# The output projection of a memory-augmented attention by column tile: 128 outputs per tile over all heads, with a block transpose into the next segment

## The chip, the cores and the metric

The kernel runs on one core of a Trainium2 chip. The metric is the device time of one execution in microseconds, lower is better. Engines are named TensorE (PE; its weight loads PEld), VectorE (DVE), ScalarE (ACT), GpSimd (POOL) and SyncE (SP, which here only issues DMAs).

## The reference, cut to what matters

Two attention branches on the same x (2048 tokens, 512 features, bf16) are mixed by a gate per token. Branch A goes through 64 segments of 32 tokens one after the other and hands 8 memory rows on:

```python
mem = mem0                                        # 8 rows
for s in range(64):
    h = concat([mem, x[32*s : 32*(s+1)]])         # 40 tokens
    q, k, v = h @ Wq, h @ Wk, h @ Wv              # 32 heads of 128
    p = softmax(where(mask, q @ k.T * scale, -1e9))
    o = einsum('hqe,hed->qd', p @ v, Wo)          # 40 rows of 512
    mem, out[s] = o[:8], o[8:]
```

Branch B is a 32-head attention of head size 16 in four blocks of 512 tokens, with a running compressive memory; it has no serial chain through A. The result is `g * A + (1 - g) * B`, with `g = sigmoid(x . gate_w)`.

So a segment of A can't begin before the first 8 output rows of the segment before are known.

## The kernel before, in words

**Phases.** The first 61 us load the inputs, transpose x into `xT` and make B's projections. After that branch A runs in 16 groups of four segments; B's attention steps, the left-over rows and the output of earlier groups are put between A's steps. Everything is unrolled.

**The order.** A segment's work is cut into units, and three written lists (`A_FIRST` for groups 0 to 2, `A_GROUP`, `A_LAST`) give the order in which units are issued; a unit that has nothing to do is skipped. Each engine works its own instructions in that order, and semaphores carry the dependencies. Names in the lists: `0.K0x` is segment 0's K projection, half b=0 of the heads, first half of the contraction; `k0` its eviction, `TK0` its transpose; `S` scores, `X` exponentials, `M` sums, `L` reciprocals, `N` and `n` norms (`n` on GpSimd), `PV`/`PL` values, `E` evictions into `OT_sb`, `W` the output projection, `H` its eviction, `F` the fold, `hm` the memory rows into the next segment's `hT`, `ax` the output rows, `xc` the copy of x into `hT`, `oL` and `qt` copies of left-over rows. `bS`, `bE`, `bP`, `bT` are B's scores, exponentials, values and late steps, `tb` and `tf` the output of an older group, `tl` its loads.

**Left-over rows.** A segment has 40 rows, of which the 32 column tiles' rows hold the 8 memory rows and the first 24 tokens. The last 8 tokens of four segments are treated together as one further tile of 32 rows: `left_units(g)` makes their K, Q and V (`KL0` ... `VL1`) for the next group while a group runs, `ol0`/`ol1` their output projection.

**Column tiles.** TensorE is used as four column tiles of 32: a stationary operand of 128 x 32 makes 32 output partitions, and four matmuls with neighbouring tiles run side by side. In `out_part` (line 1087) tile j takes head 4k+j with all 512 outputs:

```python
for k in ks:
    for j in range(4):
        matmul(pb[bk][32*j : 32*(j+1), :], lhs(4*k + j), Wo_sb[:, 4*k + j, :], ...)
```

So each tile holds a part sum over 8 of the 32 heads. `part_out` evicts the bank in two halves to f32 (`WF`, or `LN_sb` for the left-over rows), and `fold` (line 1105) adds the four parts and turns the rows into columns with small f32 matmuls against a 0/1 matrix; `w_mem` and `w_rows` evict what is needed into `hT` and `aT_st`.

**Left values.** The left-over V is evicted to `LN_sb`, block-transposed into `VTL`, turned by 16 matmuls against the identity (`vt0`, `vt1`, line 1066) and evicted into `VL`. Before group 0 all eight left units run one after the other.

Of the kernel before, what the change touches and what calls it, by code (L numbers as in the profile page):

```python
# [233 lines left out]
def build(nc, es, A_x, A_mem0, A_Wq, A_Wk, A_Wv, A_Wo, B_wq, B_wk, B_wv, B_wo, B_beta, gate_w, out, dbg=None):  # L234
# [31 lines left out]
    def alloc(stack, *specs):  # L266
        at, spans = 0, {}
        for name, shape, dt, n in specs:
# [10 lines left out]
    alloc(es, ("ident", [128, 128], BF16, 0), ("xT", [128, C, S], BF16, 0), ("hT", [128, C, SEG], BF16, 2),  # L279
# [9 lines left out]
          ("aTg", [128, C, 128], BF16, 0), ("fold", [128, SEG], F32, 0), ("VTL", [128, 4, H // 2, 8, 2], BF16, 0),  # L289
          ("WF", [128, DM], F32, 0))  # L290
    esP = ExitStack()
    in_p = alloc(esP, ("wkB", [128, C, DM], BF16, 0), ("wqB", [128, C, DM], BF16, 0), ("phK", [128, 4, DM], BF16, 0), ("etmp", [128, 512], BF16, 5),
          ("bmask", [128, 136], BF16, 0), ("mskT", [128, 2, 2, 8, 2], BF16, 0), ("mem0_sb", [128, DM], BF16, 0), ("gwr_sb", [128, 128], BF16, 0), ("beta_sb", [128, HB], BF16, 0),
# [6 lines left out]
    RT = [128, 4, H // 2, 8, 2]  # L300
    in_a = alloc(esA, ("xL", [128, C, SEG], BF16, 0), ("LN_sb", [128, 2, 512], BF16, 0), ("KTL0", RT, BF16, 0), ("QTL0", LT, BF16, 0), ("VL0", [128, 2, 512], BF16, 0),
          ("KN_sb", [128, 2, 512], BF16, 0), ("QN_sb", [128, 2, 512], BF16, 0), ("KT_sb", LT, BF16, 0), ("QT_sb", [128, H // 2, L, 2], BF16, 0),
          ("V_sb", [128, 2, 512], BF16, 0), ("P_sb", [128, 2, 224], BF16, 0), ("R_sb", [128, 2, 160], F32, 0),
          ("OT_sb", [128, H, L], BF16, 0), ("OTL", [128, H, SEG], BF16, 2), ("KTL1", RT, BF16, 0), ("QTL1", LT, BF16, 0), ("VL1", [128, 2, 512], BF16, 0),
          ("oTt", [128, 16, 32], F32, 0), ("t1_sb", [128, DM], F32, 0), ("aT_st", [128, C, 128], BF16, 2))
# [12 lines left out]
    dram("aTd", [NG, 128, C, 128])  # L318
# [97 lines left out]
def plan_const(v):  # L416
# [29 lines left out]
    def late():  # L446
# [5 lines left out]
        for n in range(2):  # L452
            gp(lambda g, n=n: g.memset(v.mskT[:, n, n, :, :], 0.0), rmt, "mskT0")
        rf = Rs("fold")
        gp(lambda g: g.memset(v.fold[:], 0.0), rf, "fold0", True)
        for j in range(4):
            sel(v.fold[:], [[-1, SEG]], ALU.not_equal, 1.0, -SEG * j, 1, rf, "fold1_%d" % j)
        for j in range(4):
            q = slice(32 * j, 32 * j + 32)
            gp(lambda g, q=q: g.memset(onesb[q, q], 1.0), rob, "onesb1_%d" % j)  # L460
            for i in range(4):
                o = (L + 16) * i
                sel(mneg[q, o + M:o + L], [[1, 32]], ALU.is_ge, NEG, M, -1, rmk, "mneg1_%d" % j)
            for n in range(2):
                row = v.mskT[q, n, n, :, :]
                for u in range(2):
                    sel(row[:, :, u], [[-1, 8]], ALU.is_ge, NEG, -16 * u - 8, 1, rmt, "mskT1_%d" % j)
                    sel(row[:, :, u], [[0, 8]], ALU.is_ge, 0.0, -16 * u - 8, 1, rmt, "mskT2_%d" % j)
                    sel(row[:, :, u], [[0, 8]], ALU.is_ge, NEG, -16 if u else 15, 1 if u else -1, rmt, "mskT3_%d" % j)
        v.late_mask = lambda: P.op("dve", lambda d: d.transpose(mneg[:, :].rearrange("p (i w) -> p i w", w=L + 16)[:, :, L:L + 16], v.mskT[:, :, :, :, :].rearrange("p n m k u -> p (n m) (k u)")),  # L470
# [4 lines left out]
def plan_warm(v):  # L475
    P, Rs, BK = v.P, v.Rs, v.BK
    v.warm = v.WF[:, :].bitcast(BF16)[:, 0:512]
# [94 lines left out]
def gate_parts(v):  # L572

    P, Rs, BK, C, NTT = v.P, v.Rs, v.BK, v.C, v.NTT
    st = {}
# [25 lines left out]
    def memory():  # L601
# [8 lines left out]
        v.evac("dve", v.hT[0][:, :, 0:v.M], v.pb16[bk][:, 0:C * v.M].rearrange("p (c t) -> p c t", t=v.M), [bk], [Rs("hTm0_0"), Rs("hTm0_1")], "memT0")  # L610
# [136 lines left out]
class BAttn:  # L747
# [178 lines left out]
A_FIRST = """  # L926
    bP bP bT bS 0.Q0x tl bE tl bE 0.Q0y 0.K0x 0.K0y 0.Q1x tb tf 0.q0 bE bT 0.qt 0.Q1y 0.K1x 0.k0 0.K1y 0.TK0 0.q1 bP 0.TQ0 bP 0.TQ1 0.k1 bS 0.V0x 0.S0
    bP bP 0.TK1 0.V0y 0.S1 0.V1x 0.X0 0.V1y 0.M0 QL1 0.X1 0.M1 bE bT 0.v1 0.L0 tbe 0.n0 0.v0 0.N0 tbe VL0 0.xc tf 0.L1 0.PV0 bT tfe 0.PL0 0.n1 KL1 bP
    0.N1 0.E0b 0.E0a 0.PV1 0.PL1 0.W0b 0.E1a 0.E1b 0.W0a 0.W1a tf 0.W1b bP VL1 bT 0.H0 0.F0 tf 0.H1 0.F1 bT tfe 0.hm0 0.hm1 QL0 tl 0.ax0 0.ax1 tf bS
    1.Q0x 1.Q0y 1.K0x 1.Q1x 1.q0 1.K0y bE 1.K1x bE 1.K1y 1.Q1y 1.qt bP 1.k0 1.TQ0 tf 0.oL 1.k1 bE bP 1.TK0 bS tl 1.TK1 bP 1.S0 1.q1 tf 1.V0x 1.TQ1 bS  # L930
    1.V1x 1.S1 bP 1.X0 tb 1.M0 bE 1.V0y 1.X1 tfe 1.M1 bT tb tb 1.L0 tfe bE 1.v0 1.V1y tf 1.N0 1.L1 bP tbe bE 1.n0 1.PV0 1.xc bE 1.n1 1.PL0 QL1e 1.E0b
    1.N1 KL0 1.v1 1.E0a 1.PV1 1.PL1 1.W0b 1.E1a 1.E1b 1.W0a bT 1.W1a tbe 1.W1b 1.H0 bS tb bT tfe 1.F0 1.H1 tl 1.oL tl 1.hm0 1.F1 1.hm1 bP 2.qt 2.Q0x
    1.ax0 2.K0x 2.Q0y tbe bT bE bT bS 1.ax1 bE 2.K0y 2.k0 2.Q1x VL1e tfe 2.Q1y bT 2.K1x 2.K1y 2.q0 2.q1 2.TQ0 2.TK0 2.S0 VL0e 2.k1 tl bP tb bP tfe
    2.TQ1 KL1e bS 2.TK1 2.V0x tb 2.X0 bS tl KL0e 2.M0 2.S1 2.V0y 2.V1x ol0 2.L0 2.X1 bP 2.M1 tbe tf 2.n0 2.V1y 2.v0 2.N0 bE 2.PV0 2.PL0 tl 2.L1 2.E0a
    2.v1 2.E0b ol1 bP 2.n1 tb 2.N1 tb 2.PV1 tfe 2.PL1 ol1e 2.W0a 2.E1a 2.E1b 2.W0b 2.W1a 2.W1b vt0 2.H0 bE bS tb tb bT tbe 2.F0 2.H1 2.hm0 2.F1 3.qt
    2.hm1 bP 2.xc 3.K0x vt0e 2.ax0 3.Q0x bP tf bP 3.K0y 3.Q0y bP tfe 3.Q1x 3.K1x 3.Q1y 2.ax1 3.q0 bS 3.k0 bP 3.K1y 3.V0x 3.q1 tl 2.oL 3.TQ0 3.TK0 3.k1
    tf 3.S0 3.X0 3.TQ1 3.TK1 bE 3.V0y 3.V1x 3.S1 3.M0 3.X1 3.V1y 3.L0 3.v0 tfe of bE 3.M1 3.v1 3.L1 3.n0 3.N0 3.PV0 3.N1 3.n1 3.PL0 3.E0a bE 3.xc bE
    3.PV1 3.PL1 3.W0a 3.E1b QL0e 3.E0b 3.E1a 3.W0b 3.W1b 3.W1a vt1 bS bE bE 3.H0 3.F0 3.H1 tl 3.F1 vt1e bP tbe 3.hm0 3.ax0 3.hm1 bS bT 3.oL tf tf ofe
    3.ax1
    """.split()  # L940
A_GROUP = """
    bE tl bE bP 0.K0x 0.Q0x 0.K0y 0.Q1x 0.Q0y 0.K1x bT 0.qt 0.K1y 0.k0 0.TK0 0.q0 0.TQ0 0.Q1y 0.V0x 0.V1x 0.S0 bE 0.k1 tb 0.q1 0.TK1 0.V0y 0.TQ1 0.X0
    0.S1 tf 0.v0 0.X1 0.M0 0.V1y 0.M1 tb 0.L0 0.L1 tbe tfe KL0 0.N0 bT 0.n0 0.v1 bT 0.PV0 bE 0.N1 0.PL0 KL1 0.xc 0.E0b 0.E0a bP 0.PV1 0.n1 0.PL1 tbe
    0.W0b 0.W0a tfe 0.E1a 0.E1b 0.W1b 0.W1a 0.H0 bE QL1 0.F0 bS bP bT 0.H1 0.F1 0.hm0 0.ax0 1.qt 0.hm1 1.K0x 1.Q0x 1.Q0y 1.K0y 1.K1x 0.ax1 1.Q1x 1.K1y
    bE 1.q0 1.Q1y 1.TQ0 1.k0 1.TK0 1.k1 1.S0 VL0 1.q1 1.TK1 bE 1.V0x 1.TQ1 0.oL 1.X0 1.S1 tfe bE 1.M0 tb tbe VL0e 1.X1 1.V0y 1.M1 1.L0 1.n0 1.V1x 1.v0
    1.N0 1.V1y 1.L1 tbe 1.PV0 1.N1 KL0e 1.PL0 tf tf 1.E0a bP bE vt0 tb tbe 1.E0b 1.v1 tf 1.n1 1.PV1 1.PL1 1.W0a 1.E1a vt0e 1.E1b 1.W0b bT 1.xc 1.W1b
    1.W1a QL1e bE bT bP 1.H0 1.H1 1.F0 tfe bS tb 1.hm0 1.F1 1.ax0 1.hm1 2.Q0x 2.Q1x 1.ax1 bE bT 2.K0x 2.Q0y bP 2.K0y 2.K1x bT 2.K1y bE tb 2.q0 2.Q1y
    bE 2.qt 2.k0 1.oL bP bP 2.TQ0 2.TK0 tb 2.S0 2.k1 2.TK1 2.q1 bS 2.TQ1 VL1 2.X0 2.M0 2.S1 bE tb 2.L0 VL1e 2.V0x 2.X1 tfe 2.V0y 2.V1x 2.n0 bE 2.M1
    2.V1y 2.N0 2.v0 bT 2.PV0 2.v1 2.L1 tbe 2.N1 2.PL0 QL0 2.E0a 2.E0b 2.n1 KL1e bP 2.PV1 2.PL1 tfe 2.W0b 2.E1b 2.W0a 2.E1a 2.W1b 2.W1a bP QL0e 2.H0
    2.H1 ol0 bE 2.F0 3.qt 2.F1 2.xc bT 2.hm0 bS 2.hm1 3.Q1x bS 2.ax1 3.Q1y 2.oL 3.K1x 3.K0x 3.q1 3.K1y 3.k1 3.Q0x 3.K0y 3.TQ1 3.TK1 3.Q0y 3.V1x bE tb  # L950
    3.S1 3.k0 3.V1y 3.q0 3.X1 3.TQ0 3.V0x 3.M1 3.L1 3.V0y 2.ax0 3.TK0 3.v1 3.N1 3.S0 3.n1 ol1 3.v0 3.X0 3.M0 3.PV1 tb 3.xc 3.PL1 tb 3.E1b 3.L0 tl vt1
    3.E1a tb 3.N0 3.n0 3.PV0 vt1e 3.PL0 ol1e 3.W1b 3.E0a tfe bT bE 3.E0b 3.W1a 3.W0b 3.W0a 3.oL of bS tfe tbe 3.H0 3.F0 3.H1 tl ofe tfe 3.F1 3.hm0 bP
    bT 3.hm1 3.ax0 3.ax1 bS
    """.split()
A_LAST = """
    bP tl bE bS bE 0.Q1x 0.K1x 0.K1y bP tb 0.Q1y bP bE 0.K0x 0.qt bP 0.K0y 0.k1 bS 0.TK1 0.Q0x 0.q1 bE 0.TQ1 bE 0.Q0y 0.S1 bS tl 0.k0 0.V1x tl 0.V0x
    0.X1 0.TK0 bE 0.M1 bE tbe 0.q0 tb tbe bS 0.TQ0 0.V1y bE bP 0.v1 0.L1 0.S0 0.V0y bE 0.n1 tf bP 0.N1 bE tf 0.X0 bE 0.M0 tl tb 0.PV1 tbe bT tf 0.PL1
    tb tbe 0.v0 tb bS tf ol0 0.L0 tl 0.E1a 0.E1b 0.xc tl tbe bT 0.n0 0.N0 0.PV0 bP 0.PL0 0.W1a bS 0.W1b tf bE tb 0.E0a 0.W0a 0.E0b 0.W0b tbe ol1 0.H0
    bT bE bP 0.F0 tbe 0.H1 0.hm0 0.F1 0.hm1 1.Q0x tf 1.Q0y bP 0.ax0 1.qt 1.K0x 1.K0y 1.K1x tb bE 1.Q1x tl 1.K1y bP bE bP bP bP bE 1.q0 tb 1.k0 1.Q1y
    tfe 1.TQ0 tb 1.TK0 tfe ol1e 1.V1x tf tf tf 1.k1 1.q1 1.V0x 1.S0 1.xc bP tfe bP bP 1.TK1 tb bT tbe bT 1.V1y 1.TQ1 bP tf 1.X0 bS bE 1.S1 1.X1 tf  # L960
    1.M0 bT 1.V0y tl bP 1.v1 0.ax1 1.v0 1.L0 2.qt 0.oL bE 1.M1 tfe 1.L1 1.N0 tb 1.N1 1.n0 1.PV0 tb tfe 1.PL0 bP 1.n1 bT 1.PV1 1.E0a 1.PL1 tfe 1.E1b bP
    bP bT 1.W0a bT bE tbe 1.E0b bE tb 1.W0b bT bP tb tb bE bE 1.E1a 1.W1b tfe tbe 1.W1a bP of bS 1.H0 bE ofe 1.F0 bT 1.H1 tb 1.F1 1.oL bS 1.hm0 bS
# [572 lines left out]
```

## Time and profile before

| | us |
|---|---|
| three runs, median | 860.64 |
| lowest and highest | 859.37 and 860.79 |
| the profiled execution | 859.77 |
| its span, first to last instruction | 858.0 |
| TensorE busy (matmuls) | 825.7 |
| ScalarE busy | 579.4 |
| VectorE busy | 572.7 |
| GpSimd busy | 254.4 |

How to read it: busy time is the union of an engine's instructions. Matmuls are pipelined and their ends are modelled, so the busy time of TensorE says that it had something to do, and not that it ran at its peak. In group lines, "xN | busy, mean of one in ns | idle before, and what ended it" stand in this order. In window lines each engine has busy time and, in brackets, the number of its instructions that lie in the window; waits for a semaphore are not in that number.

### The profile page before, as it was taken

To read this page: it belongs to the slowest core of one execution; us is meant where nothing else is said; L and a number is where in the kernel's file an instruction comes from. 1 tells how busy PE (TensorE), PEld (TensorE's weight loads), DVE (VectorE), ACT (ScalarE), POOL (GpSimd) and SP (SyncE) were. 2 spreads that over 40 slices of the span, in tenths; PEclk is the share of its full clock that TensorE was granted. 3 is DMA by queue.
4 is the path that set the end of the run, shared out by engine and by line. 5 is a ranking of instruction groups with operands and counts; after the bars stand their busy time and mean duration, and the time that the engine had idled before them with its cause. 6 is when DMAs were issued, how large, how long until landed. Compare 5 with 4: busy or idle time off the path is not lost.

```text
span 858.0 us, 51309 instructions
## 1 busy us (share of the span) xinstructions
PE 825.7 (96%) x23047; PEld 451.5 (53%) x23054; DVE 572.7 (67%) x1219; ACT 579.4 (68%) x1412; POOL 254.4 (30%) x619
## 2 busy tenths in 40 slices
PE   8998999999999999999999999999999999999997
PEld 4644454555555555555655555555555555565554
DVE  3856566565676767676776767677676767677654
ACT  5764876776677676767676676767677676767554
POOL 3611332323242232323232323233233223223210
PEclk9999999999999999999999999999999999999999
DMA  9997110000011010111111010111101011110011
GB/s 325 390 391 267 23 41 22 17 25 21 24 35 30 16 44 13 32 32 33 30 31 28 21 31 26 33 33 32 29 22 38 20 27 32 32 43 4 16 47 40
DMA packets 63587, 51.34 MB, mean 60 GB/s; under 512 B 33920, under 2 KB 59784, under 8 KB 61832
## 3 DMA queue, kind: packets, MB, share of 16 engines
q1 hardware_dynamic: 61640, 35.48, 14.4%
q10 hardware_dynamic: 1728, 12.58, 3.7%
q8 instruction: 181, 2.97, 1.4%
q14 instruction: 38, 0.31, 0.1%
HBM read 33.47 MB, written 14.57 MB: 56 GB/s over the span
## 4 chain that ended last, share of the span: by engine, by line
PE 88%; ACT 5%; DMA 3%; DVE 2%; issue 1%; POOL 0%; SPq 0%; DVEq 0%; ACTq 0%; POOLq 0%
PE ps L1007 46%; PE ps L1087 17%; PE ps L1105 4%; PE ps L1319 3%; PE ps L652 2%; PE ps L811 2%; PE ps L863 2%; PE ps L1175 2%; PE ps L1289 2%; PE ps L1258 1%; PE ps L1255 1%; DMA scr_kqd<-stgk 1%; PE ps L676 1%; DVE V_sb L365 1%; ACT R_sb L1299 1%
## 5 line engine op out<-in xcount | busy, mean ns | idle before, releaser
L837 POOL TENSOR_SCALAR_AFFINE_SELECT PT<-PT 128x256 bf16<-128x256 bf16 (+2 forms) x160 | 88.6, 554 | 271.0 <-ACT PT L830 265.9
L830 ACT ACTIVATE PT<-ps 128x1024 bf16<-128x1024 f32 x160 | 161.6, 1026 | 6.7 <-PE ps L811 5.9
L1007 PE MATMUL ps<-Wq_sb,hT 128*32 128x512 bf16 x2048 | 145.2, 380 | 0.4 <-ACT hT L363 0.3
L1007 PE MATMUL ps<-Wv_sb,hT 128*32 128x512 bf16 x2048 | 141.8, 379 | 0.8 <-issue 0.5
L1007 PE MATMUL ps<-Wk_sb,hT 128*32 128x512 bf16 x2048 | 140.6, 379 | 0.0
L1087 PE MATMUL ps<-Wo_sb,OT_sb 128*32 128x512 bf16 x2048 | 124.5, 380 | 0.3 <-issue 0.2
L363 ACT ACTIVATE OT_sb<-ps 128x320 bf16<-128x320 f32 x192 | 76.7, 434 | 50.5 <-PE ps L1331 48.0
L365 DVE CAST V_sb<-ps 128x512 bf16<-128x512 f32 x128 | 87.1, 683 | 23.4 <-PE ps L1007 22.9
L363 ACT ACTIVATE KN_sb<-ps 128x512 bf16<-128x512 f32 x128 | 77.0, 601 | 33.7 <-PE ps L1007 31.3
L1309 POOL TENSOR_TENSOR P_sb<-P_sb,R_sb 128x64 bf16<-128x64 bf16 x128 | 50.4, 394 | 143.8 <-ACT R_sb L1299 131.9
L1019 DVE STREAM_TRANSPOSE KT_sb<-KN_sb 128x256 f32<-128x256 f32 x128 | 56.3, 440 | 54.8 <-ACT KN_sb L363 54.3
L363 ACT ACTIVATE WF<-ps 128x256 f32<-128x256 f32 x128 | 42.2, 381 | 72.3 <-PE ps L1087 72.3
L1007 PEld LDWEIGHTS ps<-Wk_sb,hT 128*32 128x32 bf16 x2048 | 55.2, 97 | 49.8 <-ACT PT L830 3.0
L1007 PEld LDWEIGHTS ps<-Wq_sb,hT 128*32 128x32 bf16 x2048 | 54.1, 96 | 49.8 <-ACT hT L363 2.6
L365 DVE CAST QN_sb<-ps 128x512 bf16<-128x512 f32 x64 | 43.7, 684 | 52.7 <-PE ps L1007 52.7
L1019 DVE STREAM_TRANSPOSE QT_sb<-QN_sb 128x256 f32<-128x256 f32 x128 | 56.8, 444 | 26.3 <-ACT QN_sb L363 22.3
L1087 PEld LDWEIGHTS ps<-Wo_sb,OT_sb 128*32 128x32 bf16 x2048 | 48.5, 96 | 45.9 <-DVE OT_sb L365 8.7
L1272 ACT ACTIVATE P_sb<-ps 128x224 bf16<-128x224 f32 x128 | 45.6, 356 | 26.5 <-PE ps L1289 12.6
L365 DVE CAST LN_sb<-ps 128x512 bf16<-128x512 f32 x80 | 54.3, 678 | 9.7 <-PE ps L1007 8.7
L1007 PEld LDWEIGHTS ps<-Wv_sb,hT 128*32 128x32 bf16 x2048 | 46.4, 96 | 27.0 <-ACT KN_sb L363 2.2
L365 DVE CAST OT_sb<-ps 128x320 bf16<-128x320 f32 x64 | 31.4, 491 | 37.3 <-PE ps L1331 36.1
L1319 PEld LDWEIGHTS ps<-P_sb,V_sb 32*128 32x128 bf16 x2048 | 23.4, 91 | 51.9 <-ACT OT_sb L363 24.4
(132 smaller groups left out, 1450.8 us busy)
## 6 DMA issues: line engine op xcount, KB each, us to landing
Wk_sb<-in_A_Wk_dram ACTq DMA_DIRECT2D x4, 1024.0 KB, 7.5
scr_kqd<-stgk SPq DMA_DIRECT2D x16, 256.0 KB, 7.5
Wq_sb<-in_A_Wq_dram ACTq DMA_DIRECT2D x4, 1024.0 KB, 7.9
Wv_sb<-in_A_Wv_dram ACTq DMA_DIRECT2D x4, 1024.0 KB, 7.8
Wo_sb<-in_A_Wo_dram SPq DMA_DIRECT2D x8, 512.0 KB, 6.9
scr_vd<-V SPq DMA_DIRECT2D x16, 136.0 KB, 6.7
Vj<-scr_vd SPq DMA_DIRECT2D x32, 68.0 KB, 2.4
Wo_sb<-in_A_x_dram SPq DMA_DIRECT2D x8, 256.0 KB, 6.5
```

The costliest lines, as they stand in the source:

```text
L363: P.op("act", lambda a: a.activation(dst, src, ACT.Copy), reads=[v.rbank[k] for k in bks], writes=dres, name=name)
L365: P.op("dve", lambda d: d.tensor_copy(dst, src), reads=[v.rbank[k] for k in bks], writes=dres, name=name)
L652: ins = pe.matmul(v.pb[bk], w[:, c, f * 128:(f + 1) * 128], v.xT[:, c, 512 * sb:512 * (sb + 1)], start=(c == 0), stop=(c == C - 1))
L830: P.op("act", lambda a: a.activation(pt[:, :, :], v.ps[:, bks[0]:bks[1] + 1, :], ACT.Exp, scale=v.SCALE_B), reads=[v.rbank[b] for b in bks ...
L837: P.op("gp", lambda g: g.affine_select(mv, mv, [[0, 2], [0, len(cut)], [1, 128]], ALU.is_ge, 0.0, base=0, channel_multiplier=-1), reads=[r ...
L1007: ins = pe.matmul(pb[bk][SEG * j:SEG * (j + 1), :], lhs(c), cols(w, j) if split else w[:, 512 * j:512 * (j + 1)], start=(c == 0), stop=(c ...
L1019: P.op("dve", lambda d: d.transpose(to, src), reads=reads, writes=writes, name=name)
L1087: ins = pe.matmul(pb[bk][SEG * j:SEG * (j + 1), :], lhs(4 * k + j), Wo_sb[:, 4 * k + j, :], start=(first and k == ks[0]), stop=False, skip ...
L1105: ins = pe.matmul(pb[bk][SEG * j:SEG * (j + 1), SEG * n:SEG * (n + 1)], part[:, o:o + SEG], v.fold[:, :], start=True, stop=True, skip_grou ...
L1272: P.op("act", lambda a: a.activation(P_sb[:, b, :], pb[bk][:, 0:224], ACT.Exp, scale=SCALE), reads=[rbank[bk]], writes=[Rs("P%d" % b), Rs( ...
L1309: P.op(ENG["n"], lambda d: d.tensor_tensor(left(P_sb), left(P_sb), grp04(R_sb[:, b, :]), ALU.mult), reads=[Rs("R%d" % b)], writes=[Rs("P%d ...
L1319: ins = pe.matmul(pb[bks[j]][:, L * i:L * (i + 1)], V_sb[SEG * j:SEG * (j + 1), b, i * E:(i + 1) * E], P_sb[SEG * j:SEG * (j + 1), b, LW * ...
```

## The change

**Output projection.** Each head now goes to all four column tiles: tile j takes 128 of the 512 outputs, so that the bank holds finished sums over all heads, 32 rows of tokens by 128 outputs in each tile. A segment has 128 matmuls with 128 columns where it had 32 with 512.

```diff
             for k in ks:
-                for j in range(4):
-                    ins = pe.matmul(pb[bk][SEG * j:SEG * (j + 1), :], lhs(4 * k + j), Wo_sb[:, 4 * k + j, :],
-                                    start=(first and k == ks[0]), stop=False, skip_group_check=True)
+                for i in range(4):
+                    h = 4 * k + i
+                    for j in range(4):
+                        ins = pe.matmul(pb[bk][SEG * j:SEG * (j + 1), 0:128], lhs(h), cols(Wo_sb[:, h, :], j),
+                                        start=(first and k == ks[0] and i == 0), stop=False, skip_group_check=True)
```

**No folds.** `part_out`, `fold`, `folded` and the constant `fold` go. One eviction (ScalarE for segments, VectorE for left-over rows) writes pairs of bf16 into `WN`, and one VectorE block transpose of 32-bit elements writes them into the next segment's `hT`, which has a new layout with pairs of contraction rows next to each other:

```diff
+    def row_ev(bk, name, eng):
+        evac(eng, v.WN[:, :, :, :].rearrange("p k e u -> p k u e"), pb[bk][:, 0:128].rearrange("p (k u e) -> p k u e", u=2, e=SEG),
+             [bk], [Rs("WN")], name)
+        B.give(bk)
+
+    def out_turn(dst, writes, name):
+        src = v.WN[:, :, :, :].rearrange("p k e u -> p k (e u)").bitcast(F32)
+        P.op("dve", lambda d: d.transpose(dst, src), reads=[Rs("WN")], writes=writes, name=name)
...
-        lhs = lambda c: hT[s % 2][:, c, 0:SEG]
+        lhs = lambda c: hT[s % 2][:, c // 2, 0:4, :, c % 2].rearrange("p a q -> p (a q)")
...
+            out_turn(hT[nxt][:, :, 0::4, :, :].bitcast(F32)[:, :, :, :, 0], [Rs("hTm%d" % nxt), Rs("hTa%d" % nxt)], "hm%d" % s)
...
+            P.op("gp", lambda gq: gq.tensor_copy(dst, src), reads=[Rs("hTa%d" % nxt)], writes=[Rs("aTx%d_%d" % (par, r))], name="atx%d" % s)
```

The output rows now go from `hT` to `aT_st` by a GpSimd copy (`ax`), and `x_copy` is two GpSimd copies, one for each parity.

**Left values.** V's left-over rows are evicted without a transpose into `VNL`, stored to DRAM by one DMA and read back, turned, by four; `vt0` and `vt1` go. The rows of a left-over tile are ordered by token and then segment, so `flip_rows` for K has two half-sized transposes.

```diff
+        def turn_values():
+            P.dma(P.group("vs%d" % g, "vs"), lambda s: s.dma_start(v.vld[g].rearrange("p b a e -> p b (a e)"), v.VNL[:, :, :]),
+                  reads=[Rs("VNL0"), Rs("VNL1")], writes=[Rs("vld%d" % g)], name="stl%d" % g)
+            grp = P.group("vl%d" % g, "vl")
+            rows = v.vld[g].rearrange("(q r) b a e -> a q (r b) e", r=4)
+            for a in range(4):
+                P.dma(grp, lambda s, a=a: s.dma_start(VL[par][a:128:4, :, :], rows[a]),
+                      reads=[Rs("vld%d" % g)], writes=[Rs("VL%d_%d" % (par, b)) for b in range(2)], name="ldl%d_%d" % (g, a), scratch=True)
```

**Lists.** Sixteen lists, one a group, take the place of three; the first also holds the left units of group 0 (`iKL0` ... `iVL1e`), which ran ahead of it. The turns of group 9, as the lists have them (`...` for other units):

```diff
+    ... 0.W1a 0.E1b 0.W1b 0.H 0.hm bS ol1e bP bP 0.oL bE 1.qt bT bE 1.Q0x 1.Q0y 1.q0 ...
+    ... 1.W1a 1.W1b 1.H KL1 bS 1.hm 1.ax 2.K0x 2.Q0x ...
+    ... 2.W1a 2.W1b 2.H 2.hm 2.ax bT bS 3.xc 3.Q0x 3.Q0y bE ...
+    ... 3.W0a 3.W0b 3.W1a 3.W1b 3.H 3.hm 3.ax
```

Masks, `KTL`, `QTL` and `aT_st` change their layout to match.

## The prediction

> **What bounds the kernel now.** I read the page first, for shares and the instruction queue.
>
> ```profile
> PE 825.7 (96%) x23047; PEld 451.5 (53%) x23054; DVE 572.7 (67%) x1219; ACT 579.4 (68%) x1412; POOL 254.4 (30%) x619
> ...
> q8 instruction: 181, 2.97, 1.4%
> ```
>
> TensorE is busy 96%, no other engine over 68%. Each matmul has a weight load of its own, so TensorE runs 46,101 instructions; queue 8 brings them: 2.97 MB in 181 packets are 16 KB each, that is 256 instructions of 64 bytes.
>
> Next the groups by form on TensorE, for what the change touches.
>
> ```profile
> L1087 PE MATMUL ps<-Wo_sb,OT_sb 128*32 128x512 bf16 x2048 | 124.5, 380 | 0.3 <-issue 0.2
> L1105 PE MATMUL ps<-fold,WF 128*32 128x32 f32 x2048 | 37.1, 199 | 4.6 <-ACT WF L363 2.8 <-issue 0.9 <-DVE aT_st L365 0.3
> L1066 PE MATMUL ps<-ident,VTL 128*32 128x128 bf16 x512 | 12.9, 220 | 1.1 <-DVE VTL L1024 1.1
> ```
>
> Four column tiles run side by side, so the mean of one says little; what a run costs is the step from its first row to the next run's in the timeline of TensorE.
>
> ```profile
> 410.49 1.03 PE L1087 MATMUL ps<-Wo_sb,OTL 128*32 128x512 bf16 x16
> 411.35 0.27 PE L1289 MATMUL ps<-P_sb,onesb 128*32 128x160 bf16 x8
> ...
> 411.80 0.41 PE L1066 MATMUL ps<-ident,VTL 128*32 128x128 bf16 x16
> 412.03 1.04 PE L1175 MATMUL ps<-woB_sb,oTg 128*32 128x512 bf16 x16
> ...
> 415.19 0.45 PE L1105 MATMUL ps<-fold,LN_sb 128*32 128x32 f32 x32
> 415.57 0.40 PE L811 MATMUL ps<-QTj,KTj 32*128 32x256 bf16 x8
> ```
>
> Sixteen 512-wide matmuls take 0.86 us (a round of four 0.216), sixteen 128-wide ones 0.23 (a round 0.056 between starts), a fold of 32 takes 0.38. TensorE streams at full rate; the granted clock is 1.00.
>
> The timeline also has short waits in TensorE for which nothing visible is due ("issue"), in mid-run. Windows from 0 to two of them count instructions:
>
> ```profile
> 0.00:416.70 416.70, 398.11 (x10372) 213.66 (x10379) 273.52 (x579) 285.68 (x666) 129.67 (x338) 1.00 0.28 92
> 0.00:465.46 465.46, 445.92 (x11769) 240.93 (x11777) 307.72 (x652) 319.12 (x749) 144.35 (x371) 1.00 0.26 85
> ```
>
> Matmuls and loads between them: 2795, and 21 waits of TensorE's own (line 212): 2816, exactly 11 x 256. The waits at 77.7, 376.7, 509.8, 514.4, 709.1 and 757.5 us also lie whole multiples of 256 from these. So TensorE stands at the seam of two 16 KB blocks until the next block is there. At such a wait the packet for the block after starts 1.1 to 2.2 us later, takes 1.04 us, and the seam behind it opens at the earliest 1.2 us after it has landed. Blocks that ended in such a wait took 3.7 to 4.6 us; the quickest that did not, 2.9 (I take it that TensorE was then still working off a queue of older instructions). Cut into blocks at every alignment, the trace's steps lack 3.0 us in all to a least block time of 3.4 us, 4.5 us to 3.5; the loads' waits at seams sum to about 4. I take 3.4 us as the least time of a block of 256, bounds 3.0 and 3.7. Before, a block takes 4.6 on average and hardly meets it.
>
> **Part by part**, against the profiled execution's 859.8 us (span 858.0 and 1.8 around it; 0.9 under the median).
>
> *Folds and value turns leave TensorE.* Folds: 64 x 0.385 + 16 x 0.385 = 30.8 us; value turns 32 x 0.234 = 7.5. All of it stands in TensorE's stream: -38.3.
>
> *Wo.* Before, a segment has 32 matmuls in 8 rounds: 1.74 us. After, each head goes to all four column tiles with 128 outputs: 128 matmuls in 32 rounds, at the value turn's 0.056 1.79 us. The strided 128 columns cost nothing: Wk's and Wq's matmuls read so, and take 380 ns against Wv's 379. 64 segments and 16 left-over products, each again 128 for 32: 80 x 0.055 = +4.4.
>
> *The turn to the next segment.* Before: last Wo matmul, two evictions, folds, evictions into hT, projection.
>
> ```profile
> 550.44 0.66 ACT L363 ACTIVATE WF<-ps 128x256 f32<-128x256 f32 x2 [0.87 <-PE ps L1087]
> ...
> 551.58 0.34 ACT L363 ACTIVATE hT<-ps 128x16 bf16<-128x16 f32 x2 [0.47 <-PE ps L1105]
> ```
>
> In the shortest turns the chain takes 1.5 us from the last Wo matmul's start, and what TensorE does in it leaves some 0.7 us of waiting a group, 11 in all. After: 0.22 (drain of a 128-wide matmul) + 0.05 hop + one ScalarE eviction of 128 columns (0.275, between the rows of 64 at 0.224 and 160 at 0.300) + hop + one VectorE block transpose of 64 f32 columns (0.245: 256 take 0.444, 64 bf16 take 0.239) + hop = 0.89 us. The new lists put under it bS and two bP at the first turn of a group (0.6 us), at the others mostly one bS (0.22 to 0.32): 0.2 + 0.6 + 0.6 + 0.5 = 1.9 us less an odd left projection, 20 in all: +9.
>
> *Instruction blocks.* Added: 96 matmuls a segment and 96 a group, each with its load: 15,360 instructions; gone: 2560 folds and 512 value turns with loads, 6144. 55,300 remain, about 217 blocks. What counts is density: Wo's 256 instructions are exactly one block's worth and would run in 1.79 us. A segment has about 840: projections 192 in 5.2 us, scores 112 in 0.5, sums 32 in 0.24, values 80 in 0.47, left projections 48 in 1.3, left Wo 64 in 0.45, the other branch's rest. With these and 0.37 us of softmax waits a segment (before: 24 us) laid in the written order of groups 5 to 13, a block that starts with Wo's first instruction takes 1.9 us and lacks 1.46 to 3.4. One that starts 128 earlier has the values (80 instructions, 0.47, with 0.37 of waits), some 48 others mostly of projections (1.2) and half of Wo (0.9): 2.96, and lacks 0.45 on the mean. In the same way 64 earlier lacks 0.89, 64 later 0.68, 128 later 0.27 (behind Wo the thin projections begin: 32 instructions in 0.86 us); the eight other positions of a segment 0.67 together. Each position, 64 apart, has a weight of a quarter of a segment: 4.42 / 4 = 1.1 us a segment, 64 times = 70 us; the 4 of before are in its span already: +66. Ends: at 3.0 us some 40, at 3.7 some 105. I stay at 3.4, which the trace of before reproduces. [...]
>
> *Left values through DRAM.* Two VectorE evictions (684 ns) and two transposes a group go from VectorE. SyncE gains one store and four loads, each holding the queue 0.3 to 0.6 us; the loads wait for the store to land, and behind them stand the other branch's K and Q loads, needed only a step later. Store 1.8 + load 2.5 to landing and five issues: some 6 to 8 us, against about 10 us of list between VL1e and the next group's PL0: 0, at most 1 us a group (16).
>
> *GpSimd* gains a second copy for xT (0.25 us) and the row copies: 254 becomes some 290 us. Cover: it sits idle 132 us for the softmax reciprocals alone; if that is gone, norm_left comes 0.25 us late, up to 16 us. *VectorE and ScalarE* lose 25 and 73 us net, off the path: 0. Layouts of masks, KTL and QTL: 0.
>
> *Start and end.* From the first left projection (61.1 us) to the first segment's (70.9), 4.1 us are waits. After, Wv's landing (66.9) still gates, and the first values' DRAM round trip falls into full DMA queues (6.7 us to land): 3.4 us of waits, bounds 0 and 8: -0.7. End: one fold chain less: -1.
>
> Sum: 859.8 - 38.3 + 4.4 + 9 + 66 - 0.7 - 1 = 899.2, say **900 us**.
>
> **Rivals.** (A) *The blocks arrive in time.* Then the sum is 833 us, 3% faster. For it: the stream of TensorE does shrink by 34 us, and 2.9 us blocks passed without a wait. Against: every long "issue" wait lies on the 256 grid. It decides by the least block time: below about 2.8 us the change gains, above it the waits eat the gain. Chance 0.20.
> (B) *Part:* sequencer running ahead hides about half: 845 to 869. Chance 0.10.
> (C) *Values late too:* blocks as forecast, PL0 waits 1 us a group and GpSimd delays the norms: 900 + 32 = 932. For it: five DMAs in a row on one queue. Against: some 10 us of lead. Chance 0.05.
> (D) The change does what it says; a merged weight load for the four tiles, which would halve the added instructions, is excluded by the projections: there four neighbours share one stationary operand, and 2048 matmuls have 2048 loads. No chance given.
>
> **Numbers.** Forecast 0.65 with its own range 870 to 930 (block time 3.0 to 3.6, start and turn terms). Leaving out most of A and C, the range is 848 to 930. A difference of 0.2% is about what a measurement of this kernel can tell: faster A and a little of B, 0.22; same 0.02; slower 0.76.
>
> **What would show it.** Right: queue 8 with about 217 packets; "issue" waits before Wo's or the next rows, on the 256 grid, 60 to 80 us in all; Wo runs of 128 broken in the middle; the fold rows gone; unbroken Wo runs of 1.8 us. Turn waits on hT's transpose of some 0.5 us. Wrong: whole Wo runs back to back with blocks under 2.8 us apart, or a main wait on VL's loads, or rounds of Wo slower than 0.056.

## The result: 955 us for 861, and the profile after

The changed kernel takes 954.98 us (four runs, 951.39 to 958.17), the kernel before beside it 860.71. The ratio is 1.108, 95% interval 1.101 to 1.115. The forecast was 900 us, with a range up to 930: the direction was right, the size was not.

The page of the profile after, engines and instruction queue:

```profile
span 956.3 us, 60594 instructions
PE 833.8 (87%) x27655; PEld 504.2 (53%) x27662; DVE 561.0 (59%) x1218; ACT 533.7 (56%) x1095; POOL 284.7 (30%) x742
q8 instruction: 217, 3.56, 1.5%
```

Queue 8 brings the 217 blocks that were forecast. TensorE is now busy 87% and no other engine more than 59%: it waits, and not for them. What it waits for is in the waits after, matmuls first, then weight loads (us in total, times, longest):

```profile
PE ps L1214 <- issue: 50.7, 46, 2.0
PE ps L1138 <- DVE hT L1226: 9.7, 25, 0.7
PE ps L808 <- issue: 8.1, 6, 1.9
PE ps L1433 <- DMA VL<-scr_vld: 7.5, 1, 7.5
PE ps L1138 <- issue: 6.3, 11, 1.3
```

```profile
PEld ps L1214 <- issue: 61.6, 61, 2.2
...
PEld ps L1138 <- issue: 18.3, 39, 1.8
```

L1214 is Wo. Its "issue" waits stand in the middle of a run, as the timeline after shows:

```profile
406.28 1.97 PE L1214 MATMUL ps<-Wo_sb,OT_sb 128*32 128x128 bf16 x128
...
419.65 0.46 PE L1214 MATMUL ps<-Wo_sb,OT_sb 128*32 128x128 bf16 x20
421.51 1.24 PE L1214 MATMUL ps<-Wo_sb,OT_sb 128*32 128x128 bf16 x76 [1.40 <-issue]
...
442.49 0.22 PE L1365 MATMUL ps<-QT_sb,KTL 128*32 128x32 bf16 x7 [0.82 <-issue]
...
469.00 0.57 PE L1214 MATMUL ps<-Wo_sb,OTL 128*32 128x128 bf16 x26 [1.22 <-issue]
```

An unbroken run of 128 lasts 1.97 us with the last matmul's own 0.2, so a round is 0.056 us, as costed. The runs at 419.65 and 469.00 are cut. Windows from one cut to the next count the instructions between:

```profile
421.40:442.40 21.00, 19.31 (x637) 11.94 (x637) 13.65 (x32) 12.41 (x25) 7.98 (x19) 1.00 0.11 27
442.40:468.90 26.50, 24.38 (x893) 15.08 (x892) 16.43 (x35) 14.78 (x33) 8.32 (x21) 1.00 0.12 32
```

With TensorE's own 6 and 7 semaphore waits these are 1280 and 1792 instructions, 5 and 7 blocks of 256. Over the whole trace the weight loads' waits on this grid are 95.6 us in 96 places (before: 4.9 in 14). The new steps of the turn cost what was put down for them, 0.316 (0.275) and 0.245 us (0.245):

```profile
L364 ACT ACTIVATE WN<-ps 128x128 bf16<-128x128 f32 x64 | 20.2, 316 | 125.6 <-PE ps L1214 115.5
L1226 DVE STREAM_TRANSPOSE hT<-WN 128x64 f32<-128x64 f32 x63 | 15.5, 245 | 115.7 <-ACT WN L364 115.7
```

The second surprise is at the start: the first Wo run ends at 98.4 us, before at 83.2 (an end is here the start of the run's last matmul). SyncE's timeline after:

```profile
80.45 1.62 SPq L521 DMA_DIRECT2D Wo_sb<-in_A_Wo_dram  x2
82.11 1.26 SPq L1170 DMA_DIRECT2D scr_vld<-VNL  x1
89.37 2.50 SPq L1175 DMA_DIRECT2D VL<-scr_vld  x4
```

The store of the first left values stands behind Wo's eight loads of 0.5 MB; it is issued at 82.11, has landed at 89.3, and the loads land at 93.6.

But 8.1 of these 15.2 us are lost before there is a left value to store. The left V projection, which makes the values, starts at 74.94 us, before at 66.87:

```profile
37.32 0.69 DVE L638 SCALAR_TENSOR_TENSOR stgp<-stgk,etmp 128x512 bf16<-128x512 bf16 x1 [5.45 <-DMA scr_pQd<-stgp]
74.94 1.91 PE L1138 MATMUL ps<-Wv_sb,xL 128*32 128x512 bf16 x32 [0.43 <-DMA Wv_sb<-in_A_Wv_dram]
```

In wideplus (below), whose code up to there is that of after, the same projection starts as early as before:

```profile
66.23 1.91 PE L1138 MATMUL ps<-Wv_sb,xL 128*32 128x512 bf16 x32
```

In this execution of after, VectorE waits 5.45 us, until 37.3, for a store of branch B to land; wideplus has no such wait there. So the 8 us are a difference between executions, and not shown to come from the change. It goes both ways: narrow, which starts with the code of before, begins its left V projection at 72.6 us.

### The profile page after: what moved, and what is told of

Read it like the earlier page. It is cut to its first block, busy times and chain, and to the rows that moved or that the text cites. A ratio compares the mean times of both kernels' runs of the same rounds, so it can differ in the third digit from the quotient of the medians.

```text
span 956.3 us, 60594 instructions
## 1 busy us (share of the span) xinstructions
PE 833.8 (87%) x27655; PEld 504.2 (53%) x27662; DVE 561.0 (59%) x1218; ACT 533.7 (56%) x1095; POOL 284.7 (30%) x742
## 4 chain that ended last, share of the span: by engine, by line
PE 61%; issue 8%; ACT 3%; DVE 2%; POOL 0%; ACTq 0%; DVEq 0%
PE ps L1138 35%; PE ps L1214 14%; PE ps L1421 2%; PE ps L1276 2%; PE ps L1391 1%; PE ps L860 1%; PE ps L808 1%; PE ps L1357 1%; PE ps L1360 1%; ACT WN L364 1%; DVE hT L1226 1%; PE ps L1365 1%; PE ps L1433 1%; ACT OT_sb L364 0%; PE ps L1296 0%
## 5 line engine op out<-in xcount | busy, mean ns | idle before, releaser
L1214 PE MATMUL ps<-Wo_sb,OT_sb 128*32 128x128 bf16 x8192 | 144.6, 221 | 42.8 <-issue 41.7
L827 ACT ACTIVATE PT<-ps 128x1024 bf16<-128x1024 f32 x160 | 156.7, 1021 | 35.5 <-PE ps L808 21.5
L1214 PEld LDWEIGHTS ps<-Wo_sb,OT_sb 128*32 128x32 bf16 x8192 | 121.7, 97 | 61.6 <-issue 50.5
L1138 PE MATMUL ps<-Wq_sb,hT 128*32 128x512 bf16 x2048 | 137.7, 382 | 9.8 <-DVE hT L1226 7.0
L1138 PE MATMUL ps<-Wk_sb,hT 128*32 128x512 bf16 x2048 | 131.4, 380 | 4.3 <-DVE hT L1226 2.7
L364 ACT ACTIVATE OT_sb<-ps 128x320 bf16<-128x320 f32 x192 | 77.3, 433 | 78.4 <-PE ps L1433 70.0
L364 ACT ACTIVATE WN<-ps 128x128 bf16<-128x128 f32 x64 | 20.2, 316 | 125.6 <-PE ps L1214 115.5
L1226 DVE STREAM_TRANSPOSE hT<-WN 128x64 f32<-128x64 f32 x63 | 15.5, 245 | 115.7 <-ACT WN L364 115.7
L1138 PEld LDWEIGHTS ps<-Wv_sb,hT 128*32 128x32 bf16 x2048 | 49.6, 95 | 26.3 <-issue 4.5
L1405 DVE TENSOR_TENSOR P_sb<-P_sb,R_sb 128x160 bf16<-128x160 bf16 x128 | 43.6, 341 | 31.0 <-ACT R_sb L1401 24.6
L1398 ACT ACTIVATE R_sb<-ps 128x160 f32<-128x160 f32 x128 | 38.7, 302 | 40.8 <-PE ps L1391 40.6
```

The source lines that it names most:

```text
L364: P.op("act", lambda a: a.activation(dst, src, ACT.Copy), reads=[v.rbank[k] for k in bks], writes=dres, name=name)
L827: P.op("act", lambda a: a.activation(pt[:, :, :], v.ps[:, bks[0]:bks[1] + 1, :], ACT.Exp, scale=v.SCALE_B), reads=[v.rbank[b] for b in bks ...
L1138: ins = pe.matmul(pb[bk][SEG * j:SEG * (j + 1), :], lhs(c), cols(w, j) if split else w[:, 512 * j:512 * (j + 1)], start=(c == 0), stop=(c ...
L1214: ins = pe.matmul(pb[bk][SEG * j:SEG * (j + 1), 0:128], lhs(h), cols(Wo_sb[:, h, :], j), start=(first and k == ks[0] and i == 0), stop=Fal ...
L1226: P.op("dve", lambda d: d.transpose(dst, src), reads=[Rs("WN")], writes=writes, name=name)
L1398: P.op("act", lambda a: a.activation(R_sb[:, b, :], pb[bk][:, 224:384], ACT.Ln), reads=[rbank[bk]], writes=[Rs("R%d" % b)], name="ln%d_%d" ...
```

## The experiments

### Wo in wide matmuls again, in the kernel after (wide)

```diff
-                for i in range(4):
-                    h = 4 * k + i
-                    for j in range(4):
-                        ins = pe.matmul(pb[bk][SEG * j:SEG * (j + 1), 0:128], lhs(h), cols(Wo_sb[:, h, :], j), ...
+                for j in range(4):
+                    ins = pe.matmul(pb[bk][SEG * j:SEG * (j + 1), :], lhs(4 * k + j), Wo_sb[:, 4 * k + j, :], ...
```

> The kernel after, with Wo as 32 matmuls of 512 columns a segment, one head in each column tile, as before, and no fold: the sum over the four column tiles is left out, all else (one eviction, the block transpose, left values through DRAM, the sixteen lists) stays. TensorE loses 15,360 instructions against after, 55,317 to 39,957, some 157 blocks; the streaming is the same (8 rounds of 0.216 us for 32 of 0.056). Theory (instruction blocks): the waits at the 256 grid, 76 us ahead of matmuls and 96 ahead of weight loads in after's trace, fall to about before's 5, the drain of a 512-wide matmul costs 0.16 us more in 64 turns (10 us): 955 - 4 + 10 - (75 to 95) = 865 to 890 us. Rival 1 (the lists, the turns and the left values cost it): 940 to 965 us. Rival 2 (half and half): 900 to 930.

Measured: 854.3 us (851.3 to 859.9; before 861.6; ratio 0.992, interval 0.989 to 0.995). Page of wide:

```profile
PE 808.6 (94%) x19982; PEld 406.4 (47%) x19982; DVE 558.5 (65%) x1218; ACT 533.3 (62%) x1095; POOL 284.4 (33%) x742
q8 instruction: 157, 2.57, 1.2%
```

Turns, lists and DRAM values are still in it, and 100.7 us are gone; on the grid the weight loads wait 2.6 us in five places, 1.6 of them at the start. The 93.0 us of waits that went and the 4.4 of streaming make 97.4 of the 100.7. The extra drain of 10 us that I expected did not show: TensorE waits for `hT` 9.8 us in wide, 9.7 in after. So the added instructions cost nearly all that after loses, and more than the 75 to 95 us that I had put on them.

### Wo in narrow matmuls, in the kernel before (narrow)

```diff
+                for n in range(4):
+                    c = slice(128 * n, 128 * n + 128)
                     for j in range(4):
-                        ins = pe.matmul(pb[bk][SEG * j:SEG * (j + 1), :], lhs(4 * k + j), Wo_sb[:, 4 * k + j, :], ...
+                        ins = pe.matmul(pb[bk][SEG * j:SEG * (j + 1), c], lhs(4 * k + j), Wo_sb[:, 4 * k + j, c], ...
```

> The kernel before, with each Wo matmul of 512 columns cut into four of 128 (128 matmuls a segment for 32, one head in a column tile still); folds, value turns and both lists stay, the result is the same. TensorE gains 15,360 instructions, 46,101 to 61,461, some 240 blocks on queue 8; the streaming grows by 80 x 0.055 = 4.4 us. Theory (instruction blocks): the dense Wo run is the same as in after and the folds make it denser still, so the stalls that after has come here too: 861 + 4 + (70 to 105) = 935 to 970 us, with issue waits on the 256 grid. Rival (what after pays lies in its lists, turns or DRAM values): 861 + 4.4 = 865 us.

Measured: 1023.2 us (1017.9 to 1032.4), ratio 1.185 (1.180 to 1.190). The added instructions alone make the kernel before slower than the kernel after. Queue and weight loads' waits of narrow:

```profile
q8 instruction: 241, 3.95, 1.5%
```

```profile
PEld ps L1089 <- issue: 84.6, 61, 2.4
PEld ps L1007 <- issue: 32.8, 80, 1.8
PEld ps L1107 <- issue: 24.0, 20, 2.3
```

L1089 is Wo, L1107 the fold, L1007 the projections. On the grid the weight loads wait 148 us in all. The time is past my range (970); I take the reason to be the fold, whose dense matmuls follow Wo's there, but no run shows it alone.

### The value part alone, in the kernel before (vdram)

The layouts of masks, `KTL` and `xL`, and this in place of the value turns:

```diff
-                    dst, res = (v.VTL, "VTL%d" % b) if m == "V" else ...
+                    if m == "V":
+                        evac(ENG["VL%d" % b], v.VNL[:, b, :], pb[bk], ...)
+                        ...
+                            turn_values()     # one store, four loads
```

> The kernel before, with the value part of the change alone: left values evicted token by token, stored to DRAM and read back turned, the order of left tokens, the masks and KTL as in after, no value turns on TensorE; Wo, folds and lists as before. Theory (instruction blocks): this part saves 32 x 0.234 = 7.5 us and 1024 instructions, and costs what after shows at the start, one wait of 7.5 us of the first PV matmuls for the DRAM round trip, which stands behind Wo's loads on the queue: 853 to 861 us, no wait on the values after the first group. Rival (left values late in every group, 1 us a segment or more): 868 us or more.

Measured: 886.6 us (884.6 to 890.8), ratio 1.030 (1.026 to 1.033). The time is the rival's, the reason is not: values are waited for once, at the start.

```profile
PE ps L1328 <- DMA VL<-scr_vld: 9.2, 1, 9.2
```

In the trace the first Wo run ends at 96.1 us for 83.2, 13 us later. The other 17 are some 1.1 us a group. Of these, 12 are in short waits that the trace of before does not have: of projections and Wo's matmuls behind VectorE's evictions into `LN_sb` (4.7 and 2.9 us over the run) and of branch B's scores behind ScalarE's into `aT_st` (4.6). A left key's transpose is now two of 410 ns for one of 445, and the hand-written lists were not made for that; I take this to be the reason, but no run shows it alone. So this part is worth less than nothing in the lists of before.

### What one block costs by itself (cal)

```diff
+    for width in (512, 32, 512, 128, 512, 192, 512, 256, 512, 320):
+        rounds(pe, 32 if width == 512 else 256, width)      # a round: four tiles
+    for shift in range(4):
+        rounds(pe, 8, 384)
+        for n in range(3):
+            rounds(pe, 64, 384)
+            ins = rounds(pe, 32, 128)
```

> The kernel after, with bursts of matmuls behind its end: 1024 matmuls each (2048 instructions, 8 blocks) of 32, 128, 192, 256 and 320 columns in four column tiles, 128 matmuls of 512 columns between them; then four sets of three periods of 256 matmuls of 384 columns (10.3 us) and 128 of 128 columns (1.8 us, 256 instructions), each set 64 instructions further on the 256 grid. Nothing else runs then. By streaming alone a block takes 0.45, 1.8, 2.6, 3.5 and 4.3 us. Theory (a block takes at least T): 32, 128 and 192 columns all give the same step of a block, T, which I put at 3.4 (forecast) to 4.0 us (after's stalled blocks have a median of 3.7), 256 columns max(T, 3.5), 320 columns 4.3. In the mixed sets the dense 256 instructions cost up to 1.6 (T 3.4) or 2.2 us (T 4.0) more where they fill one block, and 0 or 1.0 where they straddle two halves. Rival (dense TensorE instructions are fetched in time): 128 columns 1.8 us a block, no long step in the mixed sets.

Measured, by windows over the five bursts of 1024 matmuls (32, 128, 192, 256, 320 columns):

```profile
961.88:987.59 25.71, 9.55 (x1028) 8.86 (x1022) 0.00 (x0) 0.00 (x0) 0.00 (x0) 0.61 0.02 4
996.34:1022.93 26.59, 15.57 (x1027) 14.52 (x1023) 0.00 (x0) 0.00 (x0) 0.00 (x0) 1.00 0.02 4
1029.85:1056.76 26.91, 22.40 (x1027) 21.17 (x1023) 0.00 (x0) 0.00 (x0) 0.00 (x0) 1.00 0.02 4
1063.67:1091.70 28.03, 28.03 (x1030) 27.90 (x1023) 0.00 (x0) 0.00 (x0) 0.00 (x0) 1.00 0.02 5
1098.61:1133.35 34.74, 34.74 (x1029) 34.74 (x1023) 0.00 (x0) 0.00 (x0) 0.00 (x0) 1.00 0.02 4
```

A matmul of 32 columns has a quarter of the columns of one of 128, and the burst takes as long: 25.71 us for 26.59. The steps from block to block are 3.47 us mostly, now and then 3.75, mean 3.5, at 32, 128 and 192 columns alike; 256 columns take 3.49 and wait for nothing, 320 take 4.35. That is a limit by count: 256 TensorE instructions, loads included, took some 3.5 us or more in these bursts. The seam between two blocks is not hidden in code this dense: in the burst of 128 columns TensorE waits 1.47 and 1.50 us at two seams in a row, 3.47 us apart.

The mixed sets went the other way: the dense 256 took 1.79 to 1.89 us, and 2.39 and 2.11 only where they filled one block. A dense block between long ones (5.2 us each) loses 0.1 to 0.6 us, and not 1.7. So the limit does not bind each block by itself; why a lone one loses less is not shown.

### Half the density (half)

```diff
-                    for j in range(4):
-                        ins = pe.matmul(pb[bk][SEG * j:SEG * (j + 1), 0:128], lhs(h), cols(Wo_sb[:, h, :], j), ...
+                    for e in range(2):
+                        j = 2 * (i % 2) + e
+                        ins = pe.matmul(pb[bk][SEG * j:SEG * (j + 1), 0:256], lhs(h), Wo_sb[:, h, 256 * e:256 * (e + 1)], ...
```

> The kernel after with Wo in 64 matmuls of 256 columns a segment: a head goes to two column tiles, two heads side by side (the sum over the two pairs of tiles is left out); the streaming is that of wide and after. TensorE has 5120 instructions more than wide and 10,240 fewer than after, some 177 blocks. A Wo run is 128 instructions in 1.73 us, half as dense as after's. Theory (a block of 256 has a least time of 3.5 us, and only what falls short of it is waited for): blocks with Wo in them fall short by little now, 0 to 0.3 us a segment: 854 to 875 us. Rival (each added TensorE instruction costs alike, 100 us for 15,360 of them): 854 + 33 = 887, 882 to 892.

Measured: 860.0 us (856.6 to 867.1), ratio 1.0005 (0.997 to 1.004); 177 blocks. A third of the added instructions cost 5.7 of the 100.7 us (7.7 when half and wide are each set against their own runs of before): a threshold, and not a price for each instruction.

### A stall of known size (wideplus)

```diff
+                for n in range(1 if len(ks) == 2 else 0):
+                    ins = pe.matmul(pb[bk][0:SEG, 128:512], lhs(4 * k), Wo_sb[:, 4 * k, 128:512], ...
```

> The kernel wide (Wo in 512 columns, the sum over the column tiles left out) with eight matmuls of 384 columns in one column tile added to each segment's Wo run, written where nothing reads: 8 x 0.16 = 1.28 us of TensorE streaming a segment in 16 instructions, 82 us in all, about what after's waits at the 256 grid add up to (81 us in steps between records). wide took 854. Theory (a stall in TensorE also throws the other engines out of step, so that it costs more than itself, as the 100 us between after and wide against 81 of waits may say): 854 + 1.25 x 82 or more, 955 or above. Rival 1 (a stall counts once): 854 + 82 = 936, 932 to 942. Rival 2 (other engines catch up meanwhile, part of it is hidden): 900 to 930.

Measured: 930.7 us (928.3 to 932.6), ratio 1.084 (1.082 to 1.086): 76.4 us for 82 of streaming (78.4 against their own runs of before), between the ranges of the two rivals. The stall in TensorE counted once here, or a little less. The theory that it costs more than itself has fallen.

### The start: without the DRAM turn (noturn), and Wo's loads later (vfirst)

```diff
 # noturn
-                        evac(ENG["VL%d" % b], v.VNL[:, b, :], pb[bk], [bk], [Rs("VNL%d" % b)], ...)
+                        evac(ENG["VL%d" % b], VL[par][:, :, :]....[:, 512 * b:512 * (b + 1)], pb[bk], [bk], ...)
 ...
 # vfirst
-        if 58 < n < 63:
+        if 58 < n < 61:
 ...
+                            if g == 0:
+                                for q in range(4, 8):
+                                    v.wo_load(q)
```

> The kernel after without the DRAM turn of the left values: VectorE evicts them straight into their tile, the store and the four loads a group are gone (the values stand in the wrong rows, the turn is left out); lists, Wo in 128 columns and the rest as in after. In after's trace the first values land only at 93.6 us, behind Wo's loads on SyncE's queue, and the first Wo run ends at 98.4 us where before's ends at 83.2. Theory (the turn costs at the start only): that end comes 7 to 11 us sooner, the pitch of a group stays at 54.5: 944 to 948 us. Rival (the five DMAs a group also hold up the other branch's loads on the queue, 1 to 1.6 us a group, as the value part alone showed in before's lists): 920 to 933 us.

> The kernel after with the last four of Wo's eight loads issued behind the first group's value store and loads; nothing else is changed, the result is the same. Theory (the first values wait for Wo's 4 MB ahead of them in the queue): the values land some 5 us sooner, the wait of 7.5 us ahead of the first left PV falls to some 2, Wo's last chunks land before they are needed: 948 to 951 us. Rival (the values wait for full DMA engines, whatever the order, or Wo then comes late): 953 to 957.

Measured: noturn 942.1 us (935.0 to 946.6), ratio 1.096 (1.091 to 1.101); vfirst 946.5 (942.0 to 949.6), ratio 1.101 (1.098 to 1.105). Both lie some 2 us below the range of their theory. The first Wo run ends at 86.6 and 87.3 us, 11.8 and 11.1 sooner than in after; but the left V projection also starts sooner, at 70.0 and 66.8 us for 74.9, ahead of anything that the two edits change. Counted from that start, the first Wo run begins 20.0 us later in after, 12.6 in noturn and 17.2 in vfirst. A group takes 53.9 and 54.2 us from Wo run to Wo run, against 54.2 in after. SyncE in vfirst:

```profile
69.44 0.32 SPq L1170 DMA_DIRECT2D scr_vld<-VNL  x1
75.13 2.50 SPq L1175 DMA_DIRECT2D VL<-scr_vld  x4
77.68 2.80 SPq L521 DMA_DIRECT2D Wo_sb<-in_A_Wo_dram  x4
```

So the DRAM turn costs 7.4 us at the start. In vfirst the first matmuls on the values start 13.3 us behind the start of the projection and not 18.7, some 5 us sooner, as the theory has it; but then TensorE waits 2.6 us for Wo's last chunks, which were to land before they are needed. The place behind Wo's loads is thus worth some 3 of the 7 us. In the sixteen new lists the five DMAs a group cost at most 0.3 us. The medians differ by more, 12.8 and 8.5 us, and what the rest is stays open; a start like that of after's trace is part of the scatter, and after's own four runs lie at 951.4, 951.9, 958.1 and 958.2 us.

### Blocks under a wait, and under DMA traffic (calwait)

```diff
+            if load:
+                for q in range(8): ...                # SyncE loads 4 MB into a dead tile
+            part(lambda pe, width=width: rounds(pe, 256, width), ...)
 ...
+                part(lambda pe: rounds(pe, 64, 384), ...)
+                if wait:
+                    P.op("act", ...)                  # a copy of the bank
+                part(lambda pe: rounds(pe, 32, 128), ...)
```

> The kernel after, with bursts behind its end again: first 1024 matmuls of 128 and 1024 of 32 columns alone (3.5 us a block of 256 instructions were measured so), then the same while SyncE loads 4 MB into a dead tile; then the mixed sets (256 matmuls of 384 columns in 10.3 us, 128 of 128 columns in 1.8 us, at four places of the 256 grid, three times each), once without a wait and once with a ScalarE copy of the bank between, on which the dense 128 wait. Question: after's waits fit a least block time of 3.7 us, quiet bursts give 3.5, and the quiet mixed sets lost only 0.1 to 0.65 us where a block of 1.8 us should have lost 1.7. Theory 1 (TensorE's sequencer runs ahead of its array behind thin code, and a semaphore wait takes that lead away): with the copy between, the dense part aligned with a block takes 1.5 us or more longer than 1.8, without it 0 to 0.7. Theory 2 (other DMA traffic makes a block take longer): under the 4 MB a block takes 4 us or more. Rival (neither): 3.5 us under load, and the same 0 to 0.7 with the copy.

Measured: with the copy between, the dense part took 1.80 us at all four places; three of the twelve periods, at one place, lost 0.5 to 0.9 us in the thin part after it. Theory 1 has fallen as it was put. The copy adds a wait of 0.6 us to each period; whether this gives the block time to come is not shown. Theory 2 holds. The timeline of TensorE in the burst of 128 columns, under the load:

```profile
1017.63 1.97 PE L1607 MATMUL ps<-Wo_sb,ident 128*32 128x128 bf16 x128 [2.80 <-issue]
1023.85 4.36 PE L1607 MATMUL ps<-Wo_sb,ident 128*32 128x128 bf16 x177 [4.24 <-issue]
```

While 4 MB came in, a block took 4.8 and 6.2 us (6.2 also in the burst of 32 columns), and 3.47 again behind it. The instruction packet itself took no longer than in the quiet burst, 0.9 to 1.0 us; but it started 2.6 to 3.9 us after the seam, where it starts 1.1 to 1.4 after it without the load. In after itself, the blocks that end in a wait of over 0.3 us have a median of 3.49 us where no other transfer ran in them, and of 4.04 in the quarter with the most (16 to 43% of the DMA engines' time). In noturn the same cut gives 3.65 and 3.58, no trend. So the 4 MB lengthened the blocks under it, from 3.47 to 4.8 and 6.2 us; how much of after's waits is due to traffic stays open.

## Why the prediction was right in kind and wrong in size

By spans, after is 98.3 us longer (956.3 for 858.0). Against the sum:

| step | forecast | measured |
|---|---|---|
| instruction blocks | +66 | +91 (95.6 less 4.9) |
| start | -0.7 (bounds 0 to 8 for the waits) | +15.2 (8.1 of it ahead of the left V projection) |
| turn waits | +9 | +19 |
| folds and value turns, Wo's streaming | -38.3 + 4.4 | -25, by difference |
| end | -1 | -1.3 |

**Instruction blocks: the step that failed, by its size.** The mechanism was right and T was too small: the largest term was put at +66 us and is +91. The sum over blocks was sound. Done on after's own trace (each block's time less its wait), the blocks lack 67 us in all to 3.4 us, 76 to 3.5 and 96 to 3.7; measured are 95.6. So the sum needs a T of 3.7 where I "stay at 3.4", and the bound at 3.7 (105) was nearest. I fitted T to a trace in which only 4 us of waits existed, and set aside the row that was nearer to the question: its blocks that ended in a wait took 3.7 to 4.6. Quiet bursts gave 3.5, and the 4 MB of calwait made it 4.8 and 6.2. 3.7 is a figure for this mix and no constant: the sum takes each block by itself, and in the mixed sets a lone dense block lost 0.1 to 0.6 us and not 1.7. After has few such long neighbours, its blocks average some 3.6 us without their waits, which may be why the sum held; no run shows it.

**Start: the round trip was put too low.** I costed the waits of the start at 3.4 us by one landing time of 6.7 us. I did not follow SyncE's queue: the store stands behind Wo's loads and lands 7.2 us after its issue, and only then are the loads issued. The first values are waited for 7.5 us in the trace, and by noturn the turn costs 7.4, just inside my bound of 8. The 8.1 us ahead of the left V projection differ between executions of the same code; they are in the row, but no step of the sum stands for them.

**Turn waits.** The last step into the projection is 0.41 us on the mean, before 0.11: 0.30 us times 64 is 19. The waits that I first wrote (1.9 us a group after, 0.7 before) give just that; the credit of 10 us for "an odd left projection" was wrong. (The 4.6 us that the folds themselves waited for before are not in the 0.11.) The shortest turn takes 0.96 us (forecast 0.89).

**Folds and turns gone.** Some 9 us of the gain are missing. The gap from Wo's end to the projection shrank from 1.82 to 1.25 us a segment, but it hid 31 other matmuls before and hides some 19 now; the rest of the segment grew by 0.38 us in wide. Which of those waits make up the 9 us is not shown.

**Right.** 217 packets; waits on the grid, before Wo above all; Wo runs cut, whole ones at 0.056 us a round; values after the first group free in the new lists (bound 16, noturn 4); GpSimd off the path (284.7 us). VectorE fell by 12 us and not 25, ScalarE by 46 and not 73, without effect. Rival A (blocks in time, 833 us) is out by the bursts; its sum without block waits was too low as well: wide, with hardly any, stands at 854. Rival C's late values are not in any trace after the first group.

No run that computes the whole result is faster than before. wide shows what is left if the dense code goes: 0.8%, with the sum over the tiles still to be paid for.

## What to carry to other kernels

Count TensorE's instructions, loads included, in windows of 256, and hold each against the 3.5 us that the quiet bursts gave: cutting Wo into matmuls of half the width cost 5.7 us over wide, into a quarter 100.7, though a segment's Wo streams for 1.73 to 1.79 us in all three. Where dense blocks followed each other, in the bursts, all that was missing to 3.47 us was paid; a lone one between long blocks lost 0.1 to 0.6 us of 1.7. Take such a limit from the blocks that did wait, and not from how little waiting there was in a kernel that hardly touched it. When a value is sent through DRAM, read the queue that it joins: its first trip may stand behind megabytes of weights, as here behind Wo's 4 MB, where the store took 7.2 us to land. And before an early delay is put down to a change, look where it begins, and in a second run of the same code.

## What was not expected of the hardware

Blocks of 256 TensorE instructions came at 3.47 us (some 3.75) at 32, 128 and 192 columns alike, and at 4.8 and 6.2 us while 4 MB were loaded at up to 380 GB/s: under that load the instruction packets started 2.6 to 3.9 us after the seam and not 1.1 to 1.4, and took 0.9 to 1.0 us as without it. And in the burst of 32 columns, where TensorE worked 9.55 of 25.71 us, the mean granted clock was 0.61, without any effect on the step of a block.
